# Moving the zero fill of the sorted tokens' buffer and the conversion steps of the output weights to other slots

## The chip, the cores and the metric

The kernel runs on one core of a Trainium2 chip. The metric is the device time of one execution in microseconds, the median of several runs. The engines are named as the profile names them: PE (TensorE, matrix products), DVE (VectorE), ACT (ScalarE), POOL (GpSimd) and SP (SyncE, which here only issues DMAs).

## What is computed

Three stages follow one another; everything is float32, with 4 sequences of 768 tokens, 8 heads of 40 channels, so 3072 tokens of 320 channels.

```python
# 1: per batch and head, a 40 x 40 state carried over 768 tokens
y[t] = r[t] @ state
Sa = state @ a[t]
state = state * w[t] - outer(Sa, b[t]) + outer(v[t], k[t])
# 2: x = y as (3072, 320)
x = ((x @ w_a) * (x @ w_b)) @ w_out                  # 320 -> 1536 -> 320
# 3: one of 8 experts per token
e = argmax(x @ w_gate);  g = softmax(x @ w_gate)[e]
out = g * (relu(x @ w1[e]) @ w2[e])                  # 320 -> 1024 -> 320
```

The weights of stage 2 come in as 64-bit floats and are split on the chip into a high and a low part.

## The kernel before

The recurrence is done in 12 chunks (c = 0 to 11) of 64 tokens. Inside a chunk it becomes matrix products and the inverse of a unit triangular matrix for each of the 32 pairs of batch and head. The body of `phase1` is a loop over the chunks, and each chunk is cut into 24 slots (i = 0 to 23). In each slot the program emits, for PE, DVE, ACT and POOL, what is to stand there, and these four engines run it in just this order. SP's order is not written out: it is chosen when the program is built, from what is ready, so that a DMA can stand far from the slot that emits it.

A chunk's slots hold work for several chunks at once: the six stages of chunk c for two pairs of batches (`stage0` to `stage5`, even slots, first pair 0 to 10, second 12 to 22), the preparation of chunks c + 1 to c + 3, and, as filling between, the up products of stage 2 for the chunk before (`MoeUp.group`, 24 a chunk, line 1084), whose result goes to memory as hT by way of two buffers uh.

What the change and the prediction's steps touch:

- The inversion `tinv` (line 667): its two operands m and xt are loaded after slot 22. Then DVE does 31 pairs of a product (tmp, line 691) and a subtraction (xt, line 697), spread over slots 2 to 16 of the next chunk by the list "tinv". After the last subtraction `end` (line 702) writes the inverse to memory (td<-xt, line 708, four DMAs) and reads it back in another layout (s<-td, lines 712 and 713, eight DMAs). `t21a` transposes it on DVE (t, line 730) and multiplies on PE (ta, line 734): first pair in slot 22, second in slot 2 of the next chunk.
- The scans of the decay (`scans`, lines 551 to 568): the first of them clamps w on DVE (line 563) in slot 16, and is mixed in among the inversion's last steps. It must come after ACT's four reads of w (`spans`, line 542, slots 15 and 16).
- The masks: POOL sets entries above the diagonal to zero in the scores (line 626, after slots 7, 8, 15 and 19) and in the products of stage3 (line 891, slots 6 and 18).
- The conversion of the output weights (`wout_steps`, line 1018, with `split64`, line 412): 15 pieces of 128 x 256. A piece takes four steps. Its first step loads the piece after it (rawo, line 1029) and does a shift on DVE (line 425) and a square on ACT (line 427); the second a bit operation on DVE (429); the third two ACT operations (435, and 437, which writes the high part into the single buffer wo) and one on DVE (438); the fourth one on DVE (440). Its rest stands at the front of the next piece's first step: two POOL operations (443 and 450) and the store of both parts, issued by POOL (1040). In the first piece's first step, two pieces are loaded. The list "wout" says in which slots of chunks 2 to 11 a step is taken; the 15 pieces end in chunk 9.
- The zero fill: the buffer xs of the sorted tokens, 6.4 MB in memory, is filled with zeros in eight parts, in chunks 2 to 9. In slot `fill - 2` POOL sets the source tile zt to zero again, and in slot `fill` a DMA on SP writes one part (lines 347 to 353).

After the loop come the down products of stage 2 with the sorting of the tokens by expert into xs, and then the experts one after another.

Of the kernel before, what the change touches and what calls it, by code (L numbers as in the profile page):

```python
# [132 lines left out]
def phase1(tc, I, cst, drm, psA, psM, ident, hT, mk_ident, wo, xs, span, tiny, down):  # L133
# [235 lines left out]
    if not down:  # L369
# [4 lines left out]

STEADY = {
    "wout": [
# [3 lines left out]
    "r0": [19, 21, 23], "r1": [7, 14, 15], "load_r": [10, 1], "score": [7, 8, 15, 19], "row": [11, 14, 22, 23], "relayout": 10,  # L380
    "load_w": 11, "span": 14, "scan": [16, 17, 20, 20, 22], "inverse": 22, "vload": [9, 20], "uload": [19, 7],

    "t21a": [22, 26], "t21b": [24, 28],
    "tinv": [0, 0, 2, 3, 5, 5, 2, 2, 5, 5, 5, 5, 5, 5, 5, 5, 3, 0, 0, 0, 0, 0, 0, 0],
    "group": 2, "fill": 17, "dsg": 2, "dxf": 1, "dtake": 2, "dh": 1, "dst": 3,
}
LAST = {"open": 21, "free": 6, "w": [1, 17], "load": [14, 16, 19], "gate": 18, "conv": [21, 22]}

# [1459 lines left out]
```

## Time and profile before

| what | us |
|---|---|
| median of three runs | 1118.22 (1117.86 to 1122.86) |
| the profiled execution, its own time | 1117.08 |
| its span in the trace | 1115.3 |
| PE busy | 982.7 (88%) |
| DVE busy | 695.0 (62%) |
| ACT busy | 584.0 (52%) |
| POOL busy | 433.5 (39%) |

The loop over the chunks lies before some 690 us of the span. In views that list groups or instructions, "out<-in" are the program's names for the tiles written and read; in a timeline, the bracket at the end of a row is the idle time before the first instruction of the row, and what ended it. PEclk is the granted clock of PE as a share of full speed.

### The profile page before, as it was taken

The numbers are of one execution on the slowest core, as the hardware profiler recorded it, in microseconds if no ns is written. First come the engines' busy times: TensorE is split into PE (matmuls) and PEld (weight loads), VectorE is DVE, ScalarE is ACT, GpSimd is POOL, SyncE is SP. The second block draws the span as 40 slices with busy tenths as digits, with TensorE's granted clock in tenths as the row PEclk, the third lists the DMA queues.
The fourth block names the chain that finished last, engine by engine and source line by source line (L and its number), as shares of the span: only waits on it lengthen the run. The fifth ranks groups of instructions, "written<-read, shape, count | busy, mean of one in ns | idle before, by whom it ended". The sixth has DMA issues, their size and how long they took to land.

```text
span 1115.3 us, 27187 instructions
## 1 busy us (share of the span) xinstructions
PE 982.7 (88%) x10402; PEld 936.8 (84%) x10402; DVE 695.0 (62%) x1843; ACT 584.0 (52%) x1373; POOL 433.5 (39%) x469
## 2 busy tenths in 40 slices
PE   4045588999998999999999999999999999999994
PEld 4044477989898989899898999999999899999994
DVE  7789689777786969796976731336667732222230
ACT  5357867665656656566655453333334354444430
POOL 4336555333423334253333113002224466666641
PEclk9656679999999999999999999989999999999997
DMA  8654444586758586686756233825557264444500
GB/s 205 153 157 96 110 127 103 155 151 166 161 153 166 156 175 149 145 172 157 151 146 127 78 91 95 234 76 166 178 179 237 87 219 143 147 142 143 158 16 16
DMA packets 218662, 158.52 MB, mean 142 GB/s; under 512 B 125269, under 2 KB 200630, under 8 KB 218524
## 3 DMA queue, kind: packets, MB, share of 16 engines
q1 hardware_dynamic: 205196, 137.33, 47.6%
q0 software_dynamic: 9808, 15.76, 5.7%
q10 hardware_dynamic: 3520, 3.61, 1.2%
q8 instruction: 84, 1.38, 0.5%
q14 instruction: 54, 0.44, 0.1%
HBM read 108.08 MB, written 44.60 MB: 137 GB/s over the span
## 4 chain that ended last, share of the span: by engine, by line
PE 52%; DVE 19%; DMA 13%; issue 5%; ACT 5%; POOL 3%; SPq 1%; POOLq 0%; DVEq 0%; ACTq 0%
PE pm L1084 15%; PE py L1221 9%; PE u L1510 6%; PE dn L1530 6%; DMA td<-xt 4%; DVE tmp L691 4%; DVE xt L697 4%; DMA s<-td 2%; PE s1p L616 2%; DMA out<-y,ids 2%; PE p L884 2%; PE pp L868 1%; PE ta L734 1%; DVE c_s L438 1%; PE px L811 1%
## 5 line engine op out<-in xcount | busy, mean ns | idle before, releaser
L891 POOL TENSOR_SCALAR_AFFINE_SELECT s<-s 64x512 f32<-64x512 f32 x96 | 82.0, 854 | 160.0 <-ACT s L889 155.6
L691 DVE TENSOR_TENSOR tmp<-m,xt 128x126 f32<-128x126 f32 (+22 forms) x372 | 115.3, 310 | 33.8 <-DMA xt<-in_one 21.0
L1084 PE MATMUL pm<-xl,wh 128*128 128x256 f32 x576 | 129.8, 307 | 1.7 <-ACT ua L1087 1.6
L1513 DVE SCALAR_TENSOR_TENSOR hl<-u,hh 128x384 fp32r<-128x384 f32 (+5 forms) x72 | 41.4, 580 | 139.2 <-ACT hh L1512 139.2
L697 DVE TENSOR_TENSOR xt<-xt,tmp 128x126 f32<-128x126 f32 (+22 forms) x372 | 115.1, 309 | 8.6
L1096 DVE TENSOR_TENSOR uh<-pm,ua 128x256 f32<-128x256 f32 x144 | 59.8, 416 | 93.7 <-PE pm L1084 51.0
L1084 PE MATMUL pm<-xh,wl 128*128 128x256 f32 x576 | 117.0, 285 | 0.0
L1084 PE MATMUL pm<-xh,wh 128*128 128x256 f32 x576 | 116.8, 285 | 0.0
L1084 PEld LDWEIGHTS pm<-xl,wh 128*128 128x128 f32 x576 | 89.1, 193 | 5.2 <-ACT ua L1087 2.2
L1221 PE MATMUL py<-wh,hl 128*128 128x328 f32 x288 | 90.8, 315 | 2.2 <-DVE hl L1211 2.2
L1221 PE MATMUL py<-wl,hh 128*128 128x328 f32 x288 | 92.0, 319 | 0.6 <-DVE wl L1192 0.6
L1084 PEld LDWEIGHTS pm<-xh,wh 128*128 128x128 f32 x576 | 91.0, 194 | 0.0
L1221 PE MATMUL py<-wh,hh 128*128 128x328 f32 x288 | 90.6, 314 | 0.0
L1084 PEld LDWEIGHTS pm<-xh,wl 128*128 128x128 f32 x576 | 90.5, 193 | 0.0
L1084 PE MATMUL pm<-xh,w 128*128 128x256 f32 x288 | 82.2, 285 | 0.0
L1084 PE MATMUL pm<-xl,w 128*128 128x256 f32 x288 | 82.1, 285 | 0.0
L1274 POOL DMA_INDIRECT xs<-xr,si x24 | 29.8, 1242 | 134.2 <-DVE acc L1269 85.6
L734 PE MATMUL ta<-t,s 32*32 32x32 f32 x768 | 23.4, 200 | 62.5 <-DVE t L730 58.7
L1063 POOL TENSOR_TENSOR xl<-xf,xh 128x384 fp32r<-128x384 f32 x24 | 24.9, 1036 | 134.8 <-ACT xh L1062 133.0
L734 PEld LDWEIGHTS ta<-t,s 32*32 32x32 f32 x768 | 18.5, 114 | 68.0 <-ACT wh L437 34.5
L1530 PE MATMUL dn<-l,hh 128*128 128x320 f32 (+3 forms) x240 | 74.8, 312 | 0.0
L1530 PE MATMUL dn<-h,hl 128*128 128x320 f32 (+3 forms) x240 | 74.0, 308 | 0.0
(238 smaller groups left out, 2831.4 us busy)
## 6 DMA issues: line engine op xcount, KB each, us to landing
hT<-uh SPq DMA_DIRECT2D x72, 256.0 KB, 2.7
hf<-hT SPq DMA_DIRECT2D x36, 512.0 KB, 3.6
r<-in_moe_w SPq DMA_DIRECT2D x8, 1280.0 KB, 6.0
r<-in_moe_w SPq DMA_DIRECT2D x8, 1024.0 KB, 7.7
bk<-in_bk SPq DMA_DIRECT2D x22, 360.0 KB, 4.8
xs<-zt SPq DMA_DIRECT2D x8, 805.0 KB, 7.7
m<-nd SPq DMA_DIRECT2D x44, 128.0 KB, 3.0
at<-in_a SPq DMA_DIRECT2D x24, 180.0 KB, 3.1
```

The costliest lines, as they stand in the source:

```text
L691: nc.vector.tensor_tensor(box[0], m[2 * s // R][:, s % (R // 2):s % (R // 2) + 1, s + 1:].to_broadcast([128, rows, n]), xt[:, :rows, s:s + ...
L697: nc.vector.tensor_tensor(xt[:, :rows, s + 1:], xt[:, :rows, s + 1:], box[0], op=ALU.subtract)
L734: nc.tensor.matmul(pa[b % 2][urow(b, R), R * h:R * h + R], s1[b % 2][urow(b, 0), h, R:C], t11[urow(b, 0), h, :], start=True, stop=True)
L891: nc.gpsimd.affine_select(out=s2t[q * C:q * C + C], in_=s2t[q * C:q * C + C], pattern=[[0, 8], [1, C]], base=0, channel_multiplier=-1, com ...
L1063: nc.gpsimd.tensor_sub(xl[:, :, bs, ts], xf, xh[:, :, bs, ts].bitcast(F32))
L1084: nc.tensor.matmul(p, l, r, start=(i == 0), stop=(i == len(seq) - 1))
L1096: nc.vector.tensor_tensor(h[:, f % 2], p, a, op=ALU.mult)
L1221: self.nc.tensor.matmul(py, self.pair[i][l][:, k, s], self.W[r][:, first + k, cols], start=(first + k == 0 and n == 0), stop=(first + k == ...
L1274: self.nc.gpsimd.indirect_dma_start(self.xs[:], bass.IndirectOffsetOnAxis(ap=si[:, i:i + 1], axis=0), xr[:, j, :], None, bounds_check=NE * ...
L1510: nc.tensor.matmul(p, l, r, start=(i == 0), stop=(i == len(seq) - 1))
L1513: nc.vector.scalar_tensor_tensor(out=hl, in0=p, scalar=0.0, in1=hh.bitcast(F32), op0=ALU.max, op1=ALU.subtract)
L1530: nc.tensor.matmul(p, l[:, q], r[:, f], start=(f == 0 and i == 0), stop=(f == len(hs) - 1 and i == 2))
```

## The change

Two entries of the table `STEADY` change. The eight steps a chunk of the conversion move from slots 6, 9, 11, 13, 15, 18, 20 and 22 to slots 1, 3, 6, 8, 10, 13, 20 and 22, in chunks 2 to 9. The fill's DMA moves from slot 17 to slot 5, and with it the setting of its source from slot 15 to slot 3.

```diff
 STEADY = {
     "wout": [
-        0, 0, 0, 0, 0, 0, 1, 0, 0, 1, 0, 1,
-        0, 1, 0, 1, 0, 0, 1, 0, 1, 0, 1, 0],
+        0, 1, 0, 1, 0, 0, 1, 0, 1, 0, 1, 0,
+        0, 1, 0, 0, 0, 0, 0, 0, 1, 0, 1, 0],
...
-    "group": 2, "fill": 17, "dsg": 2, "dxf": 1, "dtake": 2, "dh": 1, "dst": 3,
+    "group": 2, "fill": 5, "dsg": 2, "dxf": 1, "dtake": 2, "dh": 1, "dst": 3,
 }
```

## Rows read from the trace of the kernel before

**Rows 1.** Busy time by engine, 236.8 to 644.8 us; the sum of eight chunks.
```profile
sum 408.00, PE 387.76 PEld 366.25 DVE 317.55 ACT 245.76 POOL 142.65; mean PE 48.47 PEld 45.78 DVE 39.69 ACT 30.72 POOL 17.83
```
**Rows 2.** All waits of PE, 236.8 to 644.8: total us, times, longest us.
```profile
PE ta L734 <- DVE t L730: 9.8, 13, 1.5
PE py L908 <- POOL s L891: 5.8, 7, 1.0
PE ta L734 <- ACT vn L821: 2.7, 8, 0.3
PE p L884 <- ACT uv L857: 1.3, 6, 0.2
```
**Rows 3.** Timeline of SP around the end of an inversion, a chunk with a fill.
```profile
493.38 0.38 SPq L351 DMA_DIRECT2D xs<-zt  x1
495.51 2.79 SPq L708 DMA_DIRECT2D td<-xt  x4
501.89 1.32 SPq L712 DMA_DIRECT2D s<-td  x3
```
**Rows 4.** Timeline of SP at the same place of chunk 10, without a fill.
```profile
642.80 2.58 SPq L708 DMA_DIRECT2D td<-xt  x4
645.62 1.42 SPq L712 DMA_DIRECT2D s<-td  x3
```
**Rows 5.** DMA issues of the page: count, KB each, us to landing.
```profile
xs<-zt SPq DMA_DIRECT2D x8, 805.0 KB, 7.7
...
rawo<-in_moe_w_out SPq DMA_DIRECT2D x15, 256.0 KB, 3.7
```
**Rows 6.** One microsecond: us, busy PE, PEld, DVE, ACT, POOL, PEclk, DMA share, GB/s.
```profile
301.00:302.00 1.00, 1.00 (x6) 1.00 (x6) 0.76 (x2) 0.81 (x3) 0.00 (x0) 0.50 0.59 135
```
**Rows 7.** Chain that ended last: the same 16 products at three places; start, us.
```profile
300.34 3.21 PE pm L1084 x16
...
456.19 1.91 PE pm L1084 x16
...
607.99 3.35 PE pm L1084 x16
```
**Rows 8.** Busy time by engine in four microseconds of slots 5 and 6.
```profile
470.00:474.00 4.00, 4.00 (x32) 4.00 (x31) 3.90 (x11) 2.48 (x6) 1.34 (x2) 1.00 0.02 4
```
**Rows 9.** Timeline of DVE at slot 16 of two chunks.
```profile
443.10 0.54 DVE L691 TENSOR_TENSOR tmp<-m,xt 128x16 f32<-128x16 f32 x1
...
492.93 0.17 DVE L691 TENSOR_TENSOR tmp<-m,xt 128x16 f32<-128x16 f32 x1
494.32 1.06 DVE L563 TENSOR_SCALAR w<-w 120x768 f32<-120x768 f32 x1 [1.22 <-POOL c_f L443]
```
**Rows 10.** Timeline of ACT at slot 16.
```profile
494.05 0.18 ACT L542 ACTIVATION_READ_ACCUMULATOR junk<-w,wlim 120x1 f32 x1
```
**Rows 11.** Timeline of ACT at slot 6.
```profile
473.29 0.45 ACT L427 ACTIVATE c_k<-rawo 128x256 f32<-128x256 f32 x1
```
**Rows 12.** Timeline of POOL at slot 16.
```profile
494.24 0.72 POOL L450 TENSOR_TENSOR wo<-c_f,c_s 128x256 fp32r<-128x256 f32 x1
```
**Rows 13.** Waits of DVE, 184 to 644.8: total us, times, longest us.
```profile
DVE tmp L691 <- DMA xt<-in_one: 21.0, 7, 3.5
```
**Rows 14.** Timeline of SP near slot 1 of chunk 2.
```profile
203.32 0.45 SPq L1029 DMA_DIRECT2D rawo<-in_moe_w_out  x1
```
**Rows 15.** Timeline of DVE at slot 2 of chunk 2.
```profile
202.63 0.90 DVE L730 STREAM_TRANSPOSE t<-s 32x256 f32<-32x256 f32 x2
```
**Rows 16.** Timeline of PE at slot 2 of chunk 2.
```profile
204.42 0.24 PE L734 MATMUL ta<-t,s 32*32 32x32 f32 x2
```
**Rows 17.** Timeline of POOL at slot 0: the scalings.
```profile
459.32 1.84 POOL L579 TENSOR_TENSOR at<-at,w 120x384 f32<-120x384 f32 x2
```
**Rows 18.** Tile wo, time to landing: all its DMAs, and the store at 595.
```profile
DMA to landing us min/median/max: 2.8/6.0/14.3
...
DMA to landing us min/median/max: 7.2/7.2/7.2
```

## The prediction
> **What bounds the kernel now.** I read the stretch from the second inversion's end to the last one (236.8 to 644.8 us, eight chunks of some 51 us) by engine first, since all eight fills and all conversions of the output weights lie in or just before it. TensorE is busy 387.76 of 408 us [rows 1]. The list of its waits over the same stretch closes the account: 9.8 + 5.8 + 2.7 + 1.3 = 19.6 us, and 387.8 + 19.6 is 407.4 [rows 2]. So what a change gives here is one of those four waits, or it is nothing. The largest, 9.8 us in 13 waits, is ta (the product of t21a) waiting for DVE's transpose t, and that transpose waits for the inverted blocks to come back from memory.
>
> How they come back is in SyncE's timeline. The fill goes out at 493.38, the inverse's writes td<-xt from 495.51, and the first read-back s<-td only at 501.89, which waits for the writes to land: 6.4 us [rows 3]. In the chunk without a fill the same step goes from 642.80 to 645.62, 2.8 us [rows 4]. The fill has 805 KB and takes 7.7 us to land [rows 5], so it is still running when the writes start. The fill costs this chain some 3.6 us.
>
> Two of the waits cost more than their length. After them TensorE's granted clock shows 0.50, that is 1.2 instead of 2.4 GHz [rows 6], and a block of 16 products takes 3.21 and 3.35 us where it otherwise takes 1.91 [rows 7].
>
> **The change, part by part.** Nothing is added or removed: eight fills and 15 pieces with four steps each, two pieces a chunk, as before. All is a matter of place.
>
> *The fill, from slot 17 to 5.* Its memset on GpSimd moves from slot 15 to 3 and its one DMA on SyncE goes where the memset lets it; what SyncE has to issue behind it waits that long, stores hT<-uh and relayouts here. It leaves the front of td<-xt: 3.6 us less on the chain to ta. At its new place TensorE is past stage2 of the first pair; there is a hole of 4 us in which the DMA engines are 0.02 busy [rows 8], so most of a 7.7 us transfer meets little. I cost it there at nothing; the cover is that hole, and the price without it is the first rival.
>
> *The step at slot 15, to slot 10.* That step finishes one piece and begins the next: on GpSimd a subtraction, an addition and the store's issue, on ScalarE a square, on DVE a shift, on SyncE a load. At its old place it stands before the end of the inversion. DVE's product of 16 elements takes 0.54 us at 443.10 and 0.17 at 492.93; the scan's clamp (L563) waits 1.22 us and then takes 1.06, and only behind it comes the last subtraction that lets td<-xt go [rows 9]. What the clamp waits for is put down to the conversion's subtraction, but the last read of the limits on ScalarE ends at 494.05 + 0.18 = 494.23 [rows 10], 0.09 before it starts, and program order wants that read first; the square ahead of it takes 0.45 [rows 11]. GpSimd's addition runs to 494.24 + 0.72 = 494.96 [rows 12], and the clamp ends 0.42 later. With both gone I take 0.35 us off the wait and 0.5 off the clamp: 0.9 us. At slot 10 the same two operations meet the inversion's middle, where they may hold DVE as long as here: between a gain of 0 and of 0.9 I take 0.9, since the fill's 3.6 alone is more than ta needs. The Trainium skill's page SBUF — State Buffer, Who interferes with whom, says that a GpSimd operation and a DVE operation with two SBUF inputs exclude each other for the whole instruction. The two durations of the product agree; by that rule the blocking would only move, and the 0.9 would be 0.
>
> So t comes up to 3.6 + 0.9 = 4.5 us earlier, while the longest single wait for it is 1.5 [rows 2]. I take **all 9.8 us** as gone, and the two stretches at half clock with them: 1.3 + 1.4 = **2.7 us**. What is late next is py waiting for the masks of slot 18 (5.8 us), which start when ScalarE's copy is there and not when GpSimd is free. I take nothing from it; if the earlier clamp frees the masks of DVE's company it could lose half, 2.9.
>
> *The other steps* (6 to 1, 9 to 3, 11 to 6, 13 to 8, 18 to 13; 20 and 22 stay). In slots 1 to 3 DVE waits for the inversion's operand, 21.0 us in 7 chunks, 3.0 each [rows 13], which covers a shift and a bit operation. On ScalarE and DVE in slots 6 to 13 no wait of TensorE's list names them except the 0.2 us for uv, so they lie beside its products, at nothing. GpSimd has only the scalings and one subtraction near slots 1 and 10. What it costs if that cover is gone is the second rival. Loads: in the steady chunks the piece of slot 1 was loaded long before.
>
> *The first piece, in chunk 2, has no chunk before it.* Its load goes out at 203.32 [rows 14] and lands 3.7 us later [rows 5], at 207.0. Now the first shift stands in slot 1, ahead of the transposes of 202.63 on DVE [rows 15], so these end their first half at some 207.95, and ta, which starts at 204.42 [rows 16], at 208.0: **3.5 us lost, once**. Behind the same load ScalarE's first square waits in slot 1, and behind that the copies of vn, so both engines stand on it. It is 0 if SyncE's order brings the load forward, and 3.5 + 1.4 if the clock falls behind it. I take 3.5, because the load already goes straight after the loads of slot 1.
>
> Sum: -9.8 - 2.7 + 3.5 = -9.0 us. The profiled execution took 1117.08 us, 1.1 below the median of the runs, 1118.22. From 1117.1 it gives 1108.1; on the median's scale **1109.2 us**, 0.8% faster. Bounds of its own: -9.8 - 2.7 - 2.9 = -15.4 (1103) and -5.6 (1112.6).
>
> **Rivals.**
> *The queueing moves with the fill: no change.* What SyncE issued 2.1 us behind the fill came back 3.6 us late [rows 3, 4], and at slot 5 something else stands behind it. That would be the store hT<-uh. DVE would wait for it before its next write to uh; 3.6 us there would make the inversion end that much later, and of 4.5 us 0.9 stay. Over 8 chunks that saves at most 8 x 0.9 = 7.2 of the 9.8 us of waits, likelier half, 3.6; the clock's loss stays, the 3.5 is paid: 1118.1, no change. For it: the slots before are the busiest of the chunk. Against it: TensorE does not see DVE at that place. Here also belongs that the fill stays where it was, since SyncE's order isn't written out; against that, it stands right behind its memset's slot now. The Trainium skill's page DMA: Bandwidth & Descriptors, Queues, rings and completion order, speaks for this rival: it gives each issuing queue a ring of its own on each DMA engine, so that what follows on SyncE stands in line. 22%.
>
> *The store of slot 1 holds ScalarE: slower.* The buffer wo is single. The store issued in slot 1, by my estimate at 463 (GpSimd's scalings end at 461.16 [rows 17], two operations of 0.72 and the issue follow), must land before ScalarE writes wo again at the end of slot 6, where the conversion's square now stands at 473.29 [rows 11]. So it decides at a landing of about 10.3 us. The DMAs that write or read wo took 2.8 to 14.3 us, median 6.0 [rows 18]. In slot 1 it meets the inversion's operands and now the fill. At 14.3 ScalarE stands for 4.0 us with the copies of products behind it, and in 7 chunks that is 28 us against the 9.0 gained: 1137. Against it: of the eight stores that ran beside a fill before, the slowest landed in 7.2 [rows 18]. 12%.
>
> **How the numbers follow.** Forecast 66%, the first rival 22%, the slower one 12%. About 0.5% (5.6 us) is what a measurement of this kernel can tell from no change. The forecast's own range of 1103 to 1112.6 is all faster by more than that; so faster 0.66, same 0.22, slower 0.12. The range for 8 in 10 takes in the first rival and leaves out the slower one: 1103 to 1119.
>
> **What would show it.** Right: 2.8 to 3.5 us from the first td<-xt to the first s<-td in all chunks, no wait of ta for t, chunks of some 50 us, no stretch at half clock near 300 and 608, a clamp of 0.55 us, and one wait of some 3.5 us near 204. Wrong: the fill still ahead of td<-xt on SyncE; longer waits of DVE for hT<-uh; ScalarE's cast into wo starting late in slot 6; or ta's waits gone with others of the same length in TensorE's list.

## The result, and the profile after

The change makes the kernel faster by 0.8%.

| | us |
|---|---|
| before, median of 9 runs | 1117.86 (1115.22 to 1122.86) |
| after, median of 9 runs | 1108.92 (1104.72 to 1113.67) |
| ratio after / before | 0.9918, 95% interval 0.9893 to 0.9942 |
| forecast | 1109.2 (1103 to 1119) |
| the profiled execution of after, its own time | 1112.37 |
| its span in the trace | 1110.6 |

Single executions of after are spread over 9 us, so a profiled one is best read stage by stage. I cut both traces at the first td<-xt of each inversion. First chunk 2, then the eight chunks behind it, in the kernel before (the columns are those of [rows 6]):

```profile
185.40:236.78 51.38, 48.32 (x674) 45.47 (x673) 42.38 (x113) 34.36 (x89) 19.55 (x26) 1.00 0.57 146
236.78:642.80 406.02, 385.78 (x5353) 364.26 (x5352) 315.66 (x854) 245.38 (x619) 142.67 (x179) 0.99 0.67 149
```

The same two stretches after:

```profile
185.16:243.60 58.44, 49.32 (x670) 46.54 (x669) 42.46 (x114) 34.29 (x89) 19.88 (x26) 0.94 0.59 141
243.60:634.08 390.48, 382.07 (x5356) 361.46 (x5355) 310.66 (x853) 244.62 (x619) 137.01 (x178) 1.00 0.63 153
```

The eight chunks give 406.02 - 390.48 = 15.5 us, and chunk 2 takes 58.44 - 51.38 = 7.1 back: 8.5 are left at the last inversion. What lies behind it is not touched by the change; in the profiled executions of all kernels here it takes 471 to 479 us, which alone spreads the times by 8 us. So I compare kernels by their medians and by **the length of the eight chunks**.

Where the 15.5 us come from is in the list of PE's waits, 243.6 to 634.1 us of the kernel after (total us, times, longest us):

```profile
PE ta L734 <- ACT vn L821: 2.7, 8, 0.3
PE pu L817 <- ACT sg L835: 2.4, 4, 0.6
PE py L908 <- POOL s L891: 1.1, 7, 0.2
PE pm L1084 <- ACT ua L1087: 1.1, 2, 0.9
PE p L884 <- ACT uv L857: 0.8, 3, 0.3
```

Against [rows 2] the 9.8 us for the transpose t are gone, those for the masks fell from 5.8 to 1.1, and 3.5 us of waits for ScalarE (sg, ua) are new: 19.6 us became 8.1. Busy PE fell by 385.8 - 382.1 = 3.7 us, and no microsecond of these chunks shows a granted clock under 0.97 any more; before, two stretches did. 11.5 + 3.7 is 15.2 of the 15.5.

Why t is no longer late: the inverse's writes and their read-back on SP, after, and the landing of these writes in the eight chunks (min, median, max), before and then after:

```profile
443.13 2.68 SPq L708 DMA_DIRECT2D td<-xt  x4
446.43 1.29 SPq L712 DMA_DIRECT2D s<-td  x3
```
```profile
DMA to landing us min/median/max: 4.9/5.6/6.4
```
```profile
DMA to landing us min/median/max: 2.1/2.1/2.6
```

From the first write to the first read-back it is 3.3 us now; it was 6.4 with the fill ahead [rows 3] and 2.8 where there was none [rows 4].

What chunk 2 lost, in the timelines of SP, DVE, ACT and PE after, and one microsecond of the windows:

```profile
204.48 0.97 SPq L1029 DMA_DIRECT2D rawo<-in_moe_w_out  x2
205.56 0.49 SPq L351 DMA_DIRECT2D xs<-zt  x1
```
```profile
209.92 0.29 DVE L425 TENSOR_SCALAR c_f<-rawo 128x256 int32<-128x256 int32 x1 [7.45 <-DMA rawo<-in_moe_w_out]
```
```profile
209.92 0.44 ACT L427 ACTIVATE c_k<-rawo 128x256 f32<-128x256 f32 x1 [6.82 <-DMA rawo<-in_moe_w_out]
```
```profile
210.70 0.28 PE L734 MATMUL ta<-t,s 32*32 32x32 f32 x2 [6.45 <-DVE t L730]
```
```profile
210.00:211.00 1.00, 0.28 (x2) 0.18 (x2) 0.97 (x3) 0.98 (x3) 0.00 (x0) 0.50 1.18 226
```

DVE, ACT and PE all stand on the first piece's load, PE for 6.45 us. The load went out 1.2 us later than before [rows 14], as two loads back to back and the fill right behind them, and came 5.4 us after its issue. The granted clock is 0.50, which is 1.2 of 2.4 GHz, for some 7 us from 208 on.

### The profile page after: what moved, and what is told of

It is laid out like the page before. It is cut to its first block, busy times and chain, and to the rows that moved or that the text cites. A ratio compares the mean times of both kernels' runs of the same rounds, so it can differ in the third digit from the quotient of the medians.

```text
span 1110.6 us, 27225 instructions
## 1 busy us (share of the span) xinstructions
PE 981.9 (88%) x10402; PEld 936.3 (84%) x10402; DVE 690.2 (62%) x1843; ACT 582.9 (52%) x1373; POOL 428.1 (39%) x469
## 5 line engine op out<-in xcount | busy, mean ns | idle before, releaser
L891 POOL TENSOR_SCALAR_AFFINE_SELECT s<-s 64x512 f32<-64x512 f32 x96 | 76.4, 796 | 166.9 <-ACT s L889 162.8
L691 DVE TENSOR_TENSOR tmp<-m,xt 128x126 f32<-128x126 f32 (+22 forms) x372 | 119.3, 321 | 26.9 <-DMA m<-nd 18.6
L1530 PE MATMUL dn<-h,hh 128*128 128x320 f32 (+3 forms) x240 | 74.1, 309 | 0.0
L616 PE MATMUL s1p<-ablk,bk 120*128 120x192 f32 (+1 forms) x264 | 52.2, 341 | 23.5 <-ACT ablk L583 12.2
```

The source lines that it names most:

```text
L616: nc.tensor.matmul(ps[:2 * C, 3 * g * C:(3 * g + n) * C], self.bk5(c, b, g), self.ablk[b // 2][:, b % 2, g, 0:n, 0:C], start=True, stop=True)
L691: nc.vector.tensor_tensor(box[0], m[2 * s // R][:, s % (R // 2):s % (R // 2) + 1, s + 1:].to_broadcast([128, rows, n]), xt[:, :rows, s:s + ...
L891: nc.gpsimd.affine_select(out=s2t[q * C:q * C + C], in_=s2t[q * C:q * C + C], pattern=[[0, 8], [1, C]], base=0, channel_multiplier=-1, com ...
L1530: nc.tensor.matmul(p, l[:, q], r[:, f], start=(f == 0 and i == 0), stop=(f == len(hs) - 1 and i == 2))
```

## The experiments

Ratios are to the kernel before in the same series of runs, with 95% intervals. "Eight chunks" is the stretch above, in the one profiled execution. Before: 406.0; after: 390.5.

**1. Each half alone.** The kernel before with the fill moved (the edit below), and the kernel after with the same edit undone.

```diff
-    "group": 2, "fill": 17, "dsg": 2,
+    "group": 2, "fill": 5, "dsg": 2,
```

> Only the fill moves (slot 5); the conversion's steps stay. Theory (the fill alone held td<-xt up): 2.8 to 3.5 us from the first td<-xt to the first s<-td, no wait of ta for t in the eight chunks (9.8 us gone), no block at half clock there (2.7 gone), and no stall at 204 us: 12.5 us below before, 1105.4. py's waits for the masks stay near 5.8 us. Rival (the conversion's step at slot 15 holds the chain as well): ta keeps 3 us or more of waits, 1109 to 1113. Rival (the gain is the conversion's): within 2 us of before.

Measured: 1112.61 us (1110.16 to 1117.96), 0.9974 (0.9956 to 0.9992); eight chunks 399.6.

> Only the conversion's steps move; the fill stays in slot 17. Theory: td<-xt still takes 6.4 us; the clamp comes 0.9 us earlier, so of ta's 9.8 us at most 8 x 0.9 = 7.2 go, likelier 5; the start of chunk 2 loses 6.5 us of waiting and 1.5 of clock; py's waits fall by 3.7 if the steps caused them: 1117.9 - 5 - 3.7 + 8 = 1117, no change. Rival (the clamp's 0.9 is worth nothing, masks unaffected): 1126, 0.7% slower.

Measured: 1127.11 us (1122.65 to 1130.96), 1.0101 (1.0073 to 1.0128); eight chunks 406.1. PE's waits in the eight chunks of the steps alone:

```profile
PE ta L734 <- DVE t L730: 14.5, 20, 1.5
...
PE py L908 <- POOL s L891: 1.1, 7, 0.2
```

With the fill in slot 17 the steps save the masks' wait (1.1 instead of 5.8 us) and lose it on t (14.5 instead of 9.8): the chain through the fill sets the pace whatever else is freed. Chunk 2 takes 59.2 us here, much as it does after (58.4). With the fill alone, PE's waits and one of ACT's:

```profile
PE p L884 <- ACT uv L857: 3.9, 6, 0.7
PE pm L1084 <- ACT ua L1087: 3.6, 4, 1.1
...
PE py L908 <- POOL s L891: 2.7, 7, 0.5
```
```profile
ACT junk L542 <- DMA w<-in_w: 6.8, 6, 1.7
```

No wait for t is left, as forecast, but copies of ACT (uv, ua) are late: ACT stands in slot 15 for the decay w to come from memory, 6.8 us in 6 times. Before it never did; after it does for 2.5 us. Right behind two of these waits (1.1 us for ua, 0.7 for uv) the granted clock falls to 0.50 once, from 339 to 342. So the fill alone gives 406.0 - 399.6 = 6.4 of the 15.5 us.

**2. The start.** The kernel after, but chunk 2 takes its steps in the old slots.

```diff
-                more = wout.take(T["wout"][i])
+                more = wout.take(T["wout2" if c == 2 else "wout"][i])
```

> Both parts as changed, but in chunk 2 the steps keep their old slots, the first in slot 6. Theory: the 6.45 us wait of ta near 210 us and the half clock behind it (some 1.5 us) go, and all else stays: 1108.9 - 8 = 1101. Rival (the stall only stands for another wait that comes up in its place, as the first inversion or the store of uh): 1105 or more.

Measured: 1103.11 us (1099.22 to 1108.08), 0.9867 (0.9845 to 0.989); eight chunks 390.3. PE's wait for t in chunk 2 is gone; the chunk takes 54.2 us, with a half-clock stretch of 3 us at 196 in it, ahead of its slot 1. In all, the median is 5.8 us under that of after (taken in another series of runs). The eight chunks are as in after, so the two losses are separate.

**3. Why the fill delays td<-xt: its place in SyncE's line, or the DMA engines themselves.** The kernel before, with the fill issued by ScalarE in slot 17.

```diff
-                nc.sync.dma_start(
+                nc.scalar.dma_start(
```

> As before in all slots, but the fill in slot 17 is issued by ScalarE instead of SyncE. Theory A (td<-xt stands in line behind the fill on SyncE's queue): with another queue td<-xt lands in 2 to 3.5 us and ta's waits fall below 3 us: 1106 to 1109. Theory B (the sixteen DMA engines are shared, whichever queue it is): td<-xt still lands in 5 us or more, ta's waits stay at 8 us or more: 1116 to 1120. In between (lands in 3.5 to 5) both count.

Measured: 1121.92 us (1117.9 to 1127.72), 1.0034 (1.0013 to 1.0056); eight chunks 409.4. The fill on ACT's queue, the writes on SP's, and their landing in the eight chunks:

```profile
495.01 0.37 ACTq L351 DMA_DIRECT2D xs<-zt  x1
```
```profile
496.75 3.09 SPq L708 DMA_DIRECT2D td<-xt  x4
503.95 1.30 SPq L712 DMA_DIRECT2D s<-td  x3
```
```profile
DMA to landing us min/median/max: 5.3/6.2/6.7
```

The writes land as late as before (median 6.2 against 5.6), though the fill is not ahead of them on SP; it starts 1.7 us before them, where it started 2.1 before. PE waits 12.3 us for t (9.8 before), and the kernel is 0.3% slower, a little beyond what theory B had. It is the transfer that delays the writes, and not the place in SP's line.

**4. Where else the fill could stand.** The kernel of experiment 2 with the fill in slot 10.

```diff
-    "group": 2, "fill": 5, "dsg": 2,
+    "group": 2, "fill": 10, "dsg": 2,
```

> The late-start version with the fill in slot 10, outside the hole of slots 5 and 6, ahead of the load of w. Theory (the hole is what makes the fill free): the load of w waits for the fill, ScalarE's reads of w wait 1 us or more in each chunk, PE's waits for uv and ua reach 8 us or more: 1109 to 1114. Rival (anywhere but in front of td<-xt is free): 1103.

Measured: 1115.55 us (1111.69 to 1118.63), 0.9979 (0.9961 to 0.9997); eight chunks 398.5. SP issues the load of w 1.6 us behind the fill, and ACT, which has stood for it, starts on it 9.5 us later:

```profile
480.36 0.55 SPq L351 DMA_DIRECT2D xs<-zt  x1
...
481.97 0.95 SPq L522 DMA_DIRECT2D w<-in_w  x1
```
```profile
491.48 0.62 ACT L545 ACTIVATE junk<-w,wlim 120x384 bf16<-120x384 f32 x1 [0.81 <-DMA w<-in_w]
```

Five slots later the fill costs 12 us of the median, and ACT waits 6.6 us for w in the eight chunks. At slot 5, in the kernel after, it has company only from what was issued before it:

```profile
462.44 0.38 SPq L1098 DMA_DIRECT2D hT<-uh  x1
462.92 0.42 SPq L351 DMA_DIRECT2D xs<-zt  x1
469.97 0.87 SPq L773 DMA_DIRECT2D uv<-in_vt  x2
```

**5. The step in slot 15.** The kernel of experiment 2, with the step of slot 10 back in 15 and that of 13 in 18; only the first piece's steps are moved.

```diff
-        0, 1, 0, 1, 0, 0, 1, 0, 1, 0, 1, 0,
-        0, 1, 0, 0, 0, 0, 0, 0, 1, 0, 1, 0],
+        0, 1, 0, 1, 0, 0, 1, 0, 1, 0, 0, 0,
+        0, 0, 0, 1, 0, 0, 1, 0, 1, 0, 1, 0],
```

> The late-start version, with one step put back from slot 10 to 15 and its next from 13 to 18; the load of w stays ahead of the second load of a in SyncE's order. Theory (the step in slot 15 costs by itself: a square of 0.34 us ahead of ScalarE's reads, two GpSimd operations that hold DVE's clamp): 0.3 to 0.6 us a chunk on uv and the masks, 7 chunks, 1105 to 1107. Rival (only SyncE's order mattered): as the late start, 1103.

Measured: 1101.34 us (1097.7 to 1107.43), 0.9842 (0.9815 to 0.9868); eight chunks 390.8. The clamp of slot 16 (L563, here L566), its count, its duration in ns (min, median, max) and what it waited for, before:

```profile
L563 DVE TENSOR_SCALAR w<-w x6: 544/546/1065, 287.8 to 545.4; 120x768 f32<-120x768 f32 x6
...
  POOL c_f L443: 2.4, 2
```

After:

```profile
L563 DVE TENSOR_SCALAR w<-w x7: 560/560/561, 242.9 to 540.9; 120x768 f32<-120x768 f32 x7
```

With the step back in slot 15:

```profile
L566 DVE TENSOR_SCALAR w<-w x7: 773/778/797, 238.4 to 535.9; 120x768 f32<-120x768 f32 x7
...
  POOL c_f L446: 8.5, 7
```

With the step back, all seven clamps wait for the conversion, 1.2 us each in the mean, and take 0.2 us longer; before the change only two of six waited. No time is lost by it: the eight chunks are as with the late start (390.8 against 390.3), and no wait for t comes back.

**6. What in the first piece's four steps is worth 9 us.** Experiments 1 and 5 differ only in these steps: 399.6 against 390.8. In experiment 1 SP takes the loads of a and of w in another order than in the kernels before and after; here it is, and then that of after:

```profile
481.76 1.90 SPq L574 DMA_DIRECT2D at<-in_a  x2
483.89 0.33 SPq L519 DMA_DIRECT2D w<-in_w  x1
```
```profile
480.89 0.49 SPq L574 DMA_DIRECT2D at<-in_a  x1
482.11 0.35 SPq L519 DMA_DIRECT2D w<-in_w  x1
483.11 0.32 SPq L574 DMA_DIRECT2D at<-in_a  x1
```

The second load of a waits for PE to be done with its buffer, and where w stands behind it, w waits too. This is SP's wait for it in experiment 1:

```profile
SPq L574 <- PE px L802: 4.3, 5, 1.0
```

The order is chosen when the program is built, and moving steps changes it. To take the loads of a out of SP's line I gave them to another queue: to GpSimd, with the fill alone moved; to ScalarE, with the fill alone, with all steps, and with the first step alone.

```diff
-                        A.load_a(c3, pr)
+                        A.load_a(c3, pr, nc.gpsimd)
```

> The fill alone moved, and the loads of a issued by GpSimd, so that SyncE's load of w no longer stands behind them. Theory (with the fill alone, the load of w came late behind the loads of a and ScalarE's reads of w stood in front of its copies uv and ua): ScalarE's waits for w fall from 7.7 us to below 2.5, PE's waits for uv and ua from 9.1 us to some 4, 5 us below the fill alone: 1107. Rival (the conversion's step in slot 15 is the whole difference to the late start): the waits for w go but uv and ua stay near 9 us, 1111 to 1113.

Measured: 1112.33 us (1108.92 to 1117.68), 0.9948 (0.9929 to 0.9966); eight chunks 403.6. ACT's waits for w fell to 0.6 us, but GpSimd, which also makes the masks, is late now: PE waits 7.4 us for masks and 4.9 for t. So this run says nothing on the worth of w.

```diff
-                        A.load_a(c3, pr)
+                        A.load_a(c3, pr, nc.scalar)
...
-    "load_a": [18, 20],
+    "load_a": [19, 19],
```

> The kernel before with the fill in slot 5 and the two loads of a per chunk issued by ScalarE in slot 19, so that the load of w no longer stands behind the second load of a on SyncE, and GpSimd's order is left alone. Theory W (of the 12.5 us that the fill's move should bring, the fill alone brought 4.6 because ScalarE's reads of w come late, behind that load): ScalarE's waits for w under 2 us in all, TensorE's waits for uv and ua back to some 2 us, 1105 to 1108 us. Rival P (the first piece's old slots 6 to 13 themselves hold up GpSimd, DVE and ScalarE with the fill at slot 5): waits for w gone too, but those for masks, uv and ua stay at 8 us or more, 1111 to 1113.

Measured: 1114.14 us (1108.4 to 1118.01), 0.9972 (0.9951 to 0.9994); eight chunks 397.1. ACT waits 1.0 us for w, and PE's waits for uv and ua are down to 2.2; those for masks are 5.4. By its median this is no better than the fill alone.

> The changed kernel with the late start of the conversion in chunk 2, and the two loads of a issued by ScalarE in slot 19. Theory W: the load of w is ahead of the second load of a there already, so this changes nothing: 1101 to 1104. Rival P expects nothing of it either; if the loads of a stand in the way of anything else on SyncE, 1098 to 1100, and if their issue holds ScalarE up, 1105 to 1108 with new waits of TensorE for ua or uv.

Measured: 1104.99 us (1100.52 to 1105.6), 0.9895 (0.9859 to 0.993); eight chunks 389.5. Where w was free already, the other queue changes nothing.

Then two other subsets of the steps, with the loads of a on SP: the first step alone moved (6 to 1), and the first left in 6 with the next three at 8, 9 and 10.

```diff
-        0, 1, 0, 1, 0, 0, 1, 0, 1, 0, 1, 0,
-        0, 1, 0, 0, 0, 0, 0, 0, 1, 0, 1, 0],
+        0, 1, 0, 0, 0, 0, 0, 0, 0, 1, 0, 1,
+        0, 1, 0, 1, 0, 0, 1, 0, 1, 0, 1, 0],
```

> The changed kernel with the late start in chunk 2, and of the first piece's four steps only the first one moved (6 to 1; 9, 11 and 13 stay; the second piece at its old slots). In SyncE's order both loads of a stand ahead of the load of w again. Theory W: ScalarE waits for w in six or seven chunks, 6 us or more, TensorE's waits for uv and ua 6 us or more, 1110 to 1113. Rival P (it is the first step, with the addition and subtraction on GpSimd and the square, that has to leave slot 6): 1101 to 1105.

Measured: 1108.33 us (1104.5 to 1111.6), 0.9932 (0.991 to 0.9954); eight chunks 395.8. Both theories are half right. PE's and ACT's waits:

```profile
PE pm L1087 <- ACT ua L1090: 3.8, 4, 1.7
PE p L887 <- ACT uv L860: 3.5, 6, 0.7
```
```profile
ACT junk L545 <- DMA w<-in_w: 6.6, 5, 2.4
```

```diff
+        0, 0, 0, 0, 0, 0, 1, 0, 1, 1, 1, 0,
+        0, 0, 0, 1, 0, 0, 1, 0, 1, 0, 1, 0],
```

> The changed kernel with the late start in chunk 2, and the first piece's steps at slots 6, 8, 9 and 10, the second piece's at its old ones. The step of slot 6 stays; in SyncE's order the load of w stands between the two loads of a. Theory W: ScalarE's waits for w under 2 us, 1101 to 1105. Rival P: as with the fill's move alone, 1110 to 1113.

Measured: 1112.31 us (1107.02 to 1114.12), 0.9952 (0.9932 to 0.9972); eight chunks 402.6. Waits for w 4.2 us, and a new one of ACT for the store of the piece before, 5.6 us in 5 times. The time is that of the fill alone, but the new wait is a cost of this order of steps, so the run does not decide between the two theories.

The last run joins the two: the first step alone, and w freed by ScalarE's queue.

> The kernel of the run with the first step alone moved (6 to 1, late start in chunk 2), with the two loads of a issued by ScalarE in slot 19 as well, so that nothing of TensorE's stands ahead of the load of w on SyncE. The eight chunks took 390.3 us with all steps moved, 395.8 with the first alone, 397.1 with none of them but the loads of a on ScalarE, and 399.6 with none and the loads on SyncE. Theory: two causes of about the same size, the place of w in SyncE's order (5.5) and the first step in slot 6 (6.8); with both gone 390 to 392 us for the eight chunks, ScalarE's waits for w under 2 us, 1102 to 1106. Rival: the three other steps of the piece (9, 11 and 13 to 3, 6 and 8) have a worth of their own, as the loads of a on ScalarE brought only 2.5 us before: 394 to 396 us, 1107 to 1109.

Measured: 1103.1 us (1100.07 to 1107.87), 0.986 (0.9818 to 0.9901); eight chunks 389.7. Of PE's waits for ACT's late copies 1.3 us are left, and ACT has none for w:

```profile
PE p L887 <- ACT uv L860: 1.3, 6, 0.2
```

| eight chunks, us (median of the kernel) | w behind both loads of a | w free of them |
|---|---|---|
| first step in slot 6 | 399.6 (1112.61) | 397.1 (1114.14) |
| first step in slot 1 | 395.8 (1108.33) | 389.7 (1103.1) |

So the whole of the steps' share needs two things: the first step out of slot 6, and w ahead of the second load of a. The other steps may stay where they were. In all four kernels chunk 2 has its old steps.

The table holds the clock's losses too. In the eight chunks the granted clock falls to 0.50 once with the fill alone (from 339), twice with w free (from 396 and from 550), once with the first step moved (from 285), and never with both. One microsecond of the kernel with w free, in the first of its two stretches:

```profile
397.00:398.00 1.00, 1.00 (x7) 1.00 (x7) 0.94 (x4) 0.48 (x2) 0.00 (x0) 0.50 0.57 141
```

Each fall lies right behind waits of PE: in this kernel 1.4 us for masks ahead of the first, and 1.0 for masks and 0.6 for uh ahead of the second. A stretch costs 1.7 us, an estimate from the granted clock of its microseconds with PE busy all through. Without these losses the four lengths are 397.9, 393.7, 394.1 and 389.7: w alone gives 4.2, the first step alone 3.8, and both 8.2, so in these executions the two causes add. The medians say otherwise: w alone gives nothing, the first step alone 4.3 and both 9.5 us. So whether they add is open.

That SP's order makes w late is shown by its timeline, and by ACT's waits for w, which go when the loads of a leave SP's line (6.8 to 1.0 us, and 6.6 to none). What the first step costs in slot 6 is 397.1 - 389.7 = 7.4 us, of which the two stretches are 3.4; how it costs the rest is not shown. With w free, PE's waits there are again those for the masks of slot 18, up to 1.4 us each, and no run shows the path from slot 6 to them.

The fastest kernels are those with the late start and the first piece moved: 1101.3 to 1105.0 us in four forms, whose intervals overlap.

## Why the prediction was right

The time came out 0.3 us from the forecast, and the case was the forecast's own. That it is so near is luck: two errors of its terms cancel. The eight chunks were to give 9.8 + 2.7 = 12.5 us and gave 15.5, and the start was to cost 3.5 and cost 7.1. The bound of -5.6 is added up from no terms; it is the same number as what a measurement can tell from no change.

**The fill ahead of the writes, right.** All 9.8 us of waits for t are gone and the read-back comes 3.3 us after the first write. "The fill's 3.6 alone is more than ta needs" holds: with the fill alone moved no wait for t is left.

**The clock's 2.7 us, right in this execution.** Both stretches at 0.50 [rows 6, 7] are gone from the eight chunks, and busy PE fell by 3.7 us. But a wait for another engine brings the clock down as well: the kernel with the fill alone has no wait for t and still one such stretch, behind waits for ua and uv. The term needed these to stay short, which the prediction did not ask.

**The fill at slot 5 "at nothing": right, but the cover was another.** The fill went out at 462.92, 19.8 us behind the td<-xt of its chunk. The hole of [rows 8] began 25.8 us behind, which is 468.92 here. The six microseconds ahead of that place and the four of the hole, after:

```profile
462.92:468.92 6.00, 6.00 (x80) 5.65 (x79) 5.56 (x19) 3.28 (x9) 0.00 (x0) 1.00 1.10 262
468.92:472.92 4.00, 4.00 (x35) 3.87 (x36) 3.17 (x9) 3.23 (x8) 3.02 (x5) 1.00 0.37 71
```

In the hole all transfers together moved 71 GB/s, some 280 KB in 4 us by my estimate, so most of the fill's 805 KB will have gone ahead of it, where the DMA share is 1.10. PE was busy all through both, so the fill cost it nothing here. That SP had nothing more to issue until 469.97 is the likely cover; no run tests it alone. DVE's waits for the store hT rose from 15.8 to 23.4 us, as the first rival had it, but PE saw none of it. In slot 10, where the load of w follows 1.6 us behind it, the same fill costs 12 us.

**The step of slot 15 and the clamp: a rare row, and without effect.** The clamp of [rows 9] took 1.06 us behind a wait, but the median of the six before was 0.546, and only two of them waited for the conversion; the 0.9 us was read from the worst. After the change all take 0.56. Experiment 5 makes all seven wait and loses nothing; with the fill away t has time to spare. The Trainium skill's page SBUF — State Buffer, Who interferes with whom, has a GpSimd operation that reads SBUF and a DVE operation with two SBUF inputs exclude each other; by that the blocking would only move. The trace after agrees. These are DVE and POOL at the step's new place:

```profile
426.28 1.34 DVE L691 TENSOR_TENSOR tmp<-m,xt 128x133 f32<-128x133 f32 x1
427.65 0.78 DVE L697 TENSOR_TENSOR xt<-xt,tmp 128x133 f32<-128x133 f32 x1
428.47 0.29 DVE L691 TENSOR_TENSOR tmp<-m,xt 128x126 f32<-128x126 f32 x1
```
```profile
426.08 0.68 POOL L626 TENSOR_SCALAR_AFFINE_SELECT s<-s 64x512 f32<-64x512 f32 x1 [2.10 <-DVE c_s L440]
426.74 0.73 POOL L443 TENSOR_TENSOR c_f<-c_f,wo 128x256 f32<-128x256 f32 x1
427.54 0.74 POOL L450 TENSOR_TENSOR wo<-c_f,c_s 128x256 fp32r<-128x256 f32 x1
```

Two operations of the kind that takes 0.29 us beside an idle POOL take 1.34 and 0.78 here, beside a mask (L626) and the conversion's two operations: 1.5 us are lost in the middle of this inversion, more than the 0.9 that was to be won at its end.

**The other steps "at nothing", wrong.** This is the step that failed. "No wait of TensorE's list names them" was true of the trace of before, but in that trace PE's pace was set by t; with t early, the next limits show, and they are ACT's late reads of w and the masks. With the fill alone the steps in their old slots cost 9.1 of the 15.5 us, a fall of the clock by 1.7 among them. The prediction asked where a step's own instructions stand, and not what SP's order, which is chosen anew with every move, does to the loads of others.

**The masks' 5.8 us, not taken and gained.** "I take nothing from it", with 2.9 as bound; they fell by 4.7 us. Experiment 1 shows that both halves of the change do this, 1.1 with the steps alone and 2.7 with the fill alone. Against it stand the 3.5 us of new waits for sg and ua.

**The first piece's load, mis-sized.** The place and the mechanism were right, one wait of ta in chunk 2; 3.5 us were taken, "3.5 + 1.4 if the clock falls behind it". The wait was 6.45 us, and the chunk was 7.1 us longer. The load comes as two, 1.2 us later and with the fill behind it, and lands after 5.4 us rather than 3.7. Taking that start away gave 5.8 us of median.

**The rivals.** The first supposed that the queueing moves along with the fill. The waits of DVE for hT did grow by 7.6 us, but off PE's path. The Trainium skill's page DMA: Bandwidth & Descriptors, Queues, rings and completion order, was drawn on for it, for what follows in one queue's ring. Experiment 3 shows that the line is not what held td<-xt: from another queue the fill delays it as much. The same page's section Issuing engines are not separate DMA queues says just this, that transfers started by different engines run on the same 16 DMA engines and interleave, and the run agrees (landing 6.2 us against 5.6). The second rival, ScalarE held by the store of wo, did not come: ACT has no wait for wo in the trace after. It was near: the stores issued in slot 1 landed in 6.4 to 9.3 us there, where the prediction had 10.3 decide. It did come in experiment 6 with the steps at 6, 8, 9 and 10, where a store has only three slots before wo is written again: 5.6 us in 5 waits.

## What to carry to other kernels

A wait that is the largest in the bound engine's list hides the ones behind it: before calling a moved step free, ask whether it would still be free when that wait is gone. Where a compiler chooses the order of DMAs on a queue, every move can reorder others; a load that waits for nothing should not stand behind one that waits for compute, and that is seen in the queue's own timeline. And a pipelined step that moves earlier in a loop has a first pass with nothing loaded yet: give that pass its old place.

## What had not been expected

- A bulk write of 805 KB delays a small chain of DMAs by the same 3 to 4 us from either queue tried: td<-xt landed after 5.6 us in the median with the fill on SP's queue, 6.2 with it on ACT's, 2.1 with neither ahead.
- Half-clock stretches can hide that causes add: of the eight chunks, in one execution each, the two causes of experiment 6 give 2.5 and 3.8 us alone and 9.9 together, but 4.2, 3.8 and 8.2 without these stretches.
- The stall of 6.45 us in chunk 2 has a tail: the granted clock is 0.50 from 208 to 213 and 0.61 at 214, so the products from 210.7 on run at half speed for 4 us. That is at most 2 us more, by an estimate from the clock; busy PE in the chunk rose by 1.0 (49.32 against 48.32).
